# Head of a planned RWKV-attention and maxout-FFN kernel: scale factors on other engines, zeroing inside the list, one more chunk with corner products

## The chip, the cores and the metric

One core of one Trainium2 chip runs the whole program. The metric is device microseconds for one execution. Three timed executions of the kernel before took 390.78, 393.11 and 394.20 us; the median is 393.11 us. PE is TensorE, DVE is VectorE, ACT is ScalarE, POOL is GpSimd, and SP is SyncE, which issues most of the DMAs.

## What is computed

The inputs are r, k and v of shape (4, 8, 768, 48): batch, heads, time steps, head size. Per head there are a decay `w` and a bonus `u`. The output of the recurrence goes through a feed-forward net that takes a maximum of three projections:

```python
for t in range(S):
    cur = einsum('bhd,bhe->bhde', u[None] * kt, vt)
    y[:, :, t] = einsum('bhd,bhde->bhe', rt, state + cur)
    state = w[None, :, :, None] * state + einsum('bhd,bhe->bhde', kt, vt)
x = y.transpose(0, 2, 1, 3).reshape(3072, 384)
h = maximum(maximum(x @ w1, x @ w2), x @ w3)      # 384 -> 768
return h @ w_out                                  # 768 -> 384
```

## The kernel before

**Chunks.** The 768 steps are cut into NCH = 12 chunks of C = 64 steps. For a chunk the recurrence becomes four groups of small products, each done for two halves q = 0, 1 of the heads: `scores` (keys against queries, line 536), `keys` (the update of the state, line 586), `values` (the output, line 607), and for the first WHOLE = 2 chunks also `bonus` (line 550) and `flipped` (keys turned from feature to token layout, line 560). The output of a chunk goes as fp16 high and low parts into a tile x; six small DMAs (`x_last`, line 632) move the rest of its rows into place. Then `ffn(c)` (line 1007) does for 256 tokens 18 projections of 9 matmuls (`up`, line 656) and 3 of 18 matmuls (`down`, line 681); all of these are the matmuls of line 651.

**Precision.** Chunks 0 and 1 use fp32 operands in pieces of 64x64 (line 531). Later chunks split each operand into a high and a low fp16 part and use three products. The operands lie in `Block` tiles (line 409): per half-split s and unit u a 128-column field, of which the left 48 or 64 columns hold two heads, one in the upper and one in the lower 64 partitions. Chunks 2 and 3 (c < CORNERS = 4) multiply the two corners apart: two 64x64 matmuls for each product (line 524). From chunk 4 on, a DMA (`spread`, line 420, two issues for each block) copies a dense block into a block-diagonal one, and one 128x128 matmul does both heads (line 521). The rest of each block must be zero for that, so all 16 blocks are zeroed by POOL at the head (line 415), behind two zeroings of `ztop` (line 331) and ahead of one of `state` (line 439).

**Head.** Powers of the decay are made on DVE by scans (line 366). From them come, all on DVE, the row scales `sc` and `wrt` (lines 370 to 373), the chunk decay `wc` with two multiples `wcv` and `wck` (lines 376, 378, 390), `uw` (380), a diagonal matrix `dg` (382) and, on the list, `tkf` (line 387). `wu`, `cst` and the first inputs are issued by SP, `ut` by ACT.

**Weights.** The eight weight tiles come as 64-bit words: a DMA into one of three `raw64` buffers (line 323), then ACT (`tops`, line 340), DVE (`convert`, 344), ACT (`round_up`, 347) and DVE (`leave`, 350). Feed-forward block f needs weight f.

**Order.** From line 829 on all work is put on a list by `do(due, engine, cost, ...)`. `Plan.order` (line 171) runs a small model of the engines, PE's clock and the DMA lanes, and for each engine picks the ready entry of the least due time. Each entry's due time is shifted by the table SHIFT (line 79), by kind of work and by one of five stages; stage 0 holds due times under 0, stage 1 those from 0 to 1, and so on. The last call gives the time at which each engine is free (line 1083). The result is a fixed order of instructions on each engine; each engine runs its own in order. STIRS = 30 entries of three matmuls on zeros (line 647) keep PE's clock up where the model sees nothing else for PE. The order of before cannot be read from the table by eye; on the chip it is what the trace shows.

Of the kernel before, what the change touches and what calls it, by code (L numbers as in the profile page):

```python
# [26 lines left out]
U = 8  # L27
WHOLE = 2
CORNERS = 4
# [42 lines left out]
class Plan:  # L72
# [4 lines left out]
    BEFORE, BEHIND, PHASE, LANES = 1.5, 1.0, 1.4, 8  # L77
    CLASSES = (0.0, 1.0, 2.0, 10.0)
    SHIFT = {
        "sp feat": (3.37, -2.28, 2.83, -0.27, 0),  # L80
        "sp tok": (-0.37, -1.28, 2.64, 0.03, 0),
        "dve tkf": (0, 0.35, 0, 0, 0),
        "pe turned": (0, -0.88, 0, 0, 0),
        "act tkt": (0, -2.47, 0, 0, 0),
        "dve kT": (-0.62, -26.75, 0, 0, 0),
        "dve rT": (1.01, -35.26, -13.5, 0, 0),
        "act ru": (1.08, 1.39, 0, 0, 0),
        "pe bo": (-1.74, -0.21, 0, 0, 0),
        "dve am": (0, -0.03, 0.19, 2.29, 8.79),
        "pe sc": (6.74, 6.37, 4.36, -0.11, 0.12),  # L90
        "pe va": (-1.39, -2.73, -1.75, -0.08, 0),
        "act xh": (1.82, -0.83, 0.07, -0.97, -3.12),
        "dve xl": (0.58, 0, -2.36, -1.28, 1.02),
        "sp x3": (-1.49, -1.21, 0.13, -4.67, -1.28),
        "act xsq": (0, 0.01, 0, 2.16, -1.69),
        "pe stir": (0, -4.85, -11.53, -2.89, 0),
        "sp word": (2.21, 2.24, 0, 0, 0),
        "act ztop": (4.76, 27.48, 0, 0, 0),
        "dve word": (0, -2.64, 0, 0, 0),
        "act his": (3.42, 1.73, 0, 0, 0),  # L100
        "dve lo": (5.68, 7.43, 0, 0, 0),
        "pe kp": (5.05, -0.04, 0, 0, 0),
        "act kt": (-0.02, 0.84, 0, 0, 0),
        "pe ke": (-7.14, 6.21, -1.73, 0.35, 0),
        "act state": (0, -0.01, 0, 0, 0),
        "act sq": (0, 0.88, -7.89, 10.42, 25.44),
        "dve sd": (0, -0.87, 0, 0, 0),
        "dve state": (0.34, -0.75, -2.69, 4.27, 0),
        "act sdh": (4.06, 29.93, 3.51, 1.17, 0),
        "dve sdl": (-1.07, 0, 0.16, -0.97, 0),  # L110
        "pe up": (0, 23.33, 26.76, 0, 0.29),
        "act m": (4.63, 8.82, 0.44, 3.37, 1.6),
        "dve m": (0.55, -34.44, -6.62, -1.08, 1.37),
        "act hh": (-7.43, -4.42, -2.95, -0.81, -0.62),
        "pool hl": (6.4, -5.49, -7.62, -1.14, 0),
        "dve hl": (0, -2.26, 0.19, -0.23, 6.97),
        "pe dn": (0, 15.92, 0.15, 0.16, -7.02),
        "act io": (0, 1.07, -1.56, -0.11, 0.2),
        "sp io": (0, -0.8, -1.65, 0.71, 5.84),
        "act kdh": (0, -1.01, 0, -0.76, 4.34),  # L120
        "dve kdl": (0, 25.83, -3.45, -0.82, 0),
        "act rh": (0, -2.72, -12.01, 2.55, 0),
        "dve rl": (0, -0.6, 0, -4.47, 0),
        "dve a": (0, -2.22, 24.73, -7.12, -0.01),
        "act am": (0, -1.68, -2.12, 0, 0),
        "act ah": (0, 4.54, -7.22, -2.31, -3.79),
        "dve al": (0, -3.09, -4.17, -4.93, 4.72),
        "dve kdec": (0, 17.36, 44.29, 0, 0),
        "act ktdh": (0, 0.89, -1.64, -2.36, 0),
        "dve ktdl": (0, -3.21, -2.6, 0.42, 0),  # L130
        "act vdh": (0, 0, -14.62, 1.62, -3.2),
        "dve vdl": (0, 0, -2.03, -0.03, -0.05),
        "pool kT": (0, 0, -4.45, 18.88, 0),
        "pool rT": (0, 0, -2.66, 20.23, 3.89),
        "pool am": (0, 0, -3.01, 1.47, 1.83),
        "pool kdec": (0, 0, -10.33, 11.92, 0),
        "sp kb": (0, 0, 0, -6.2, 0.59),
        "sp ktb": (0, 0, 0, -1.92, 0),
# [1010 lines left out]
```

## Time and profile before

| | |
|---|---|
| median of the three runs | 393.11 us |
| the profiled execution's own time | 390.22 us |
| its span, first to last instruction | 388.2 us |
| PE busy | 375.1 us, 97% |
| DVE busy | 243.0 us, 63% |
| ACT busy | 244.3 us, 63% |
| POOL busy | 185.2 us, 48% |
| mean granted clock of PE | 0.993 |
| DMA | 77.23 MB, mean 199 GB/s |

The busy share is a mean over a head, a steady part and a tail with different limits, and PE's busy time holds the stirring matmuls too. What an edit is worth has to be read in the stage that it touches: views by stretches of time, the timeline of one engine, and the chain of waits that ended last.

### The profile page before, as it was taken

Reading aid. Unit: us, or ns where it says so; the run is one execution under the profiler, and the core shown is the slowest. Engines: PE = TensorE matmul, PEld = TensorE weight load, DVE = VectorE, ACT = ScalarE, POOL = GpSimd, SP = SyncE. Lnnn points to the kernel's source line nnn. Section 1 sums busy time; section 2 is a strip of 40 time slices with the busy share of each in tenths; the row PEclk is TensorE's granted clock in tenths of the full one; section 3 lists DMA queues with packets and bytes.
Section 4 is the critical chain, followed back from the end, with each engine's and each line's share of the span. In section 5 each row is a group of like instructions: output and inputs, shape, how many; then the busy total and the mean of one; then the engine's idle time right before and its main releaser. Section 6 shows DMA issues by size and latency. Waiting matters only on the chain.

```text
span 388.2 us, 13560 instructions
## 1 busy us (share of the span) xinstructions
PE 375.1 (97%) x5652; PEld 337.8 (87%) x5652; DVE 243.0 (63%) x464; ACT 244.3 (63%) x618; POOL 185.2 (48%) x187
## 2 busy tenths in 40 slices
PE   6998999899999999999999999999999999999993
PEld 4877988788889999999999999999999999998883
DVE  7397999868568597558557557456467466232350
ACT  3478986587547566566566566566556865696621
POOL 9600032359975683673673683674673550020110
PEclk8999999999999999999999999999999999999999
DMA  8866673324852994994994996994994994903201
GB/s 273 342 206 248 207 281 116 138 82 143 231 186 88 298 251 125 288 299 134 276 300 156 279 234 163 300 284 128 305 256 114 279 253 104 293 24 144 77 2 49
DMA packets 27989, 77.23 MB, mean 199 GB/s; under 512 B 4881, under 2 KB 12561, under 8 KB 26897
## 3 DMA queue, kind: packets, MB, share of 16 engines
q1 hardware_dynamic: 27776, 76.19, 66.1%
q8 instruction: 46, 0.75, 0.9%
q14 instruction: 23, 0.18, 0.2%
q10 hardware_dynamic: 144, 0.10, 0.1%
HBM read 38.38 MB, written 4.72 MB: 111 GB/s over the span
## 4 chain that ended last, share of the span: by engine, by line
PE 91%; POOL 4%; DVE 1%; ACT 1%; issue 1%; DVEq 0%; POOLq 0%
PE psm L651 72%; PE psv L521 8%; PE psa L521 3%; PE psv L524 2%; PE psv L531 2%; PE psm L647 1%; PE psa L531 1%; PE psa L524 1%; PE psa L565 1%; POOL ztop L331 1%; ACT am L497 1%; POOL ktd L415 0%; POOL vd L415 0%; POOL kd L415 0%; POOL sb L415 0%
## 5 line engine op out<-in xcount | busy, mean ns | idle before, releaser
L651 PEld LDWEIGHTS <-w 128*128 128x128 f16 x2592 | 250.2, 98 | 29.6 <-issue 0.7
L651 PE MATMUL psm<-x,w 128*128 128x256 f16 x1944 | 219.7, 273 | 0.0
L679 POOL TENSOR_TENSOR hl<-m,hh 128x256 f16<-128x256 f32 x60 | 44.6, 745 | 130.2 <-ACT hh L673 125.1
L670 DVE SCALAR_TENSOR_TENSOR m<-psm,m 128x256 f32<-128x256 f32 x144 | 60.2, 419 | 60.6 <-PE psm L651 52.5
L673 ACT CAST hh<-m 128x256 f16<-128x256 f32 x72 | 29.0, 402 | 56.2 <-DVE m L670 55.8
L651 PE MATMUL psm<-hh,w 128*128 128x256 f16 x432 | 56.3, 273 | 0.5 <-issue 0.5
L466 POOL TENSOR_TENSOR feat<-feat,wrt 128x512 f32<-128x512 f32 x36 | 49.1, 1376 | 7.0 <-DMA feat<-in_feat_dram 7.0
L485 POOL TENSOR_TENSOR am<-tok,u_sb 128x384 f32<-128x384 f32 x18 | 20.8, 1157 | 45.1 <-DVE al L584 45.1
L449 ACT ACTIVATE junk<-tok 128x384 bf16<-128x384 f32 x72 | 37.4, 520 | 3.3 <-DMA tok<-in_tok_dram 2.1
L666 ACT ACTIVATE m<-psm 128x256 f32<-128x256 f32 x72 | 27.2, 378 | 14.0 <-PE psm L651 12.7
L651 PE MATMUL psm<-hl,w 128*128 128x256 f16 x216 | 33.4, 273 | 0.0
L628 DVE SCALAR_TENSOR_TENSOR x<-psv,x 112x512 f16<-112x512 f32 x24 | 16.5, 688 | 22.6 <-ACT x L624 22.1
L624 ACT ACTIVATE x<-psv 112x512 f16<-112x512 f32 x24 | 14.3, 594 | 15.4 <-PE psv L521 14.4
L521 PE MATMUL psv<-rh,sb 128*128 128x64 f16 x256 | 23.6, 193 | 0.0
L521 PE MATMUL psv<-ah,vb 128*128 128x64 f16 x256 | 23.6, 193 | 0.0
L521 PE MATMUL psv<-al,vb 128*128 128x64 f16 x128 | 22.7, 193 | 0.0
L521 PE MATMUL psv<-rl,sb 128*128 128x64 f16 x128 | 22.7, 193 | 0.0
L499 POOL TENSOR_TENSOR am<-cs,a 128x512 f32<-128x512 f32 x18 | 20.0, 1114 | 3.4 <-DVE a L490 3.3
L490 DVE TENSOR_REDUCE a<-am 128x8 f32<-128x384 f32 x20 | 11.0, 549 | 16.9 <-POOL am L486 16.9
L521 PEld LDWEIGHTS <-vb 128*128 128x128 f16 x384 | 21.1, 98 | 0.4
L574 DVE COPY_PREDICATED am<-cs,psa 128x512 f32<-128x512 int32 x24 | 17.7, 736 | 5.6 <-PE psa L521 5.0
L696 ACT ACTIVATE io<-psm 128x256 f32<-128x256 f32 x36 | 13.4, 381 | 11.1 <-PE psm L651 11.0
(119 smaller groups left out, 579.2 us busy)
## 6 DMA issues: line engine op xcount, KB each, us to landing
tok<-in_tok_dram SPq DMA_DIRECT2D x26, 576.0 KB, 6.3
feat<-in_feat_dram SPq DMA_DIRECT2D x24, 512.0 KB, 4.6
raw<-in_ws_dram SPq DMA_DIRECT2D x6, 1152.0 KB, 7.1
out_dram<-io SPq DMA_DIRECT2D x36, 128.0 KB, 4.8
vb<-vd SPq DMA_DIRECT2D x16, 256.0 KB, 6.9
sb<-sd SPq DMA_DIRECT2D x16, 256.0 KB, 6.9
kb<-kd SPq DMA_DIRECT2D x16, 256.0 KB, 6.6
vb<-vd SPq DMA_DIRECT2D x16, 248.0 KB, 6.8
```

The costliest lines, as they stand in the source:

```text
L449: nc.scalar.activation(out=junk[:, 0:U * D].rearrange("p (u d) -> p u d", u=U), in_=src, func=AF.Square, scale=scale, accum_out=stat[:, ki ...
L466: helper(c).tensor_tensor(out=t[n], in0=t[n], in1=tb, op=ALU.mult)
L485: helper(c).tensor_tensor(out=w.rearrange("p (g b) d -> p g b d", g=2), in0=t["r"], in1=by_token(u_sb, q), op=ALU.mult)
L499: helper(c).tensor_tensor(out=t["a"], in0=eye.unsqueeze(1).broadcast_to([P, U, C]), in1=t.pop("sum").unsqueeze(2).broadcast_to([P, U, C]), ...
L521: nc.tensor.matmul(out=ps[:, i, :], lhsT=block[k].on[a][i], rhs=prods[k](b, i), **flags)
L574: nc.vector.copy_predicated(out=t["a"], mask=strict.unsqueeze(1).broadcast_to([P, U, C]), data=t.pop("sc"))
L628: nc.vector.scalar_tensor_tensor(out=x_part(x, 1, q), in0=ps, scalar=sc_x(c), in1=x_part(x, 0, q), op0=ALU.mult, op1=ALU.subtract)
L651: nc.tensor.matmul(out=ps, lhsT=a, rhs=b, start=first and n == 0, stop=last and n == len(prods) - 1)
L666: nc.scalar.mul(out=m, in_=ps, mul=by)
L670: nc.vector.scalar_tensor_tensor(out=m, in0=ps, scalar=by, in1=m, op0=ALU.mult, op1=ALU.max)
L673: nc.scalar.copy(out=h[0][:, f, :], in_=m)
L679: lows_by(c, f).tensor_tensor(out=h[1][:, f, :], in0=m, in1=h[0][:, f, :], op=ALU.subtract)
```

## The change

It has six parts.

1. **Loads.** `wu` and `cst` are issued on ACT's queue instead of SP's, ahead of `ut`.
2. **Scale factors.** `sc` is scaled by a `scalar_tensor_tensor` with a vector of ones instead of a `tensor_scalar`. `wc`, `uw` and `dg` are made by POOL, `wcv` and `wck` by ACT. `tkf` takes the buffer of `ru`. The scaling of `u_sb` is an entry on the list. The scaled copy of the state after chunk 0 moves from DVE to ACT.
3. **Zeroing.** `state` is no longer zeroed. Blocks are zeroed by 14 entries on POOL's list, and of the dense blocks only the columns that nothing else writes. Spreads wait for all of these.
4. **Corners.** CORNERS goes from 4 to 5, so chunk 4 uses corner products and no spreads.
5. **The list's model.** It adds TURN = 0.095 to the cost of a PE entry when it changes between corner products and full ones, and lowers some costs for it. Scores of chunks 0 and 1 come behind the bonus, values of the second half behind those of the first, and the projections of a chunk behind all of the chunk before. `ah` and `al` get two buffers.
6. **The table.** All of SHIFT is new, and the engines are taken as free at other times.

```diff
-CORNERS = 4
+CORNERS = 5
...
+            if e == "pe" and p["corner"] != corner:
+                corner = p["corner"]
+                cost += self.TURN
...
-    nc.sync.dma_start(out=wu_sb, in_=wu)
+    nc.scalar.dma_start(out=wu_sb, in_=wu)
...
+    nc.scalar.dma_start(out=cs, in_=cst)
...
-    nc.vector.tensor_scalar(out=sc, in0=sc, scalar1=SC_R, scalar2=None, op0=ALU.mult)
+    nc.vector.scalar_tensor_tensor(out=sc, in0=sc, scalar=SC_R, in1=one4, op0=ALU.mult, op1=ALU.mult)
...
-    nc.vector.tensor_copy(out=wc, in_=pw[:, :, C])
-    nc.vector.tensor_scalar(out=wcv, in0=wc, scalar1=SC_V, scalar2=None, op0=ALU.mult)
-    nc.vector.tensor_tensor(out=uw, in0=uf_sb, in1=w_sb, op=ALU.mult)
+    nc.gpsimd.tensor_tensor(out=wc, in0=pw[:, :, C], in1=one4, op=ALU.mult)
+    nc.gpsimd.tensor_tensor(out=uw, in0=uf_sb, in1=w_sb, op=ALU.mult)
...
-    nc.vector.tensor_tensor(out=dg, ...)
+    nc.gpsimd.tensor_tensor(out=dg, ...)
+    nc.scalar.mul(out=wcv, in_=wc, mul=SC_V)
+    nc.scalar.mul(out=wck, in_=wc, mul=SC_KT / SC_R)
...
     def both():
+        tkf = work.tile([P, U, C], F32, name="ru").rearrange("p (g h) s -> p g h s", h=2)
...
-            nc.gpsimd.memset(t.bitcast(F32), 0.0)
+            self.blank = self.dense.bitcast(F32)[:, :, :, w // 2:]
...
-    nc.gpsimd.memset(state, 0.0)
...
+            dma(due, lambda: spread(nc.sync, dst, src), 2.4, reads=[*keys, *(("pad", n) for n in range(14))], writes=[name], n=2)
...
-            do(due + 0.06, "dve", 0.5, lambda: nc.vector.tensor_scalar(out=state1[q], in0=sf, ...
+            do(due + 0.06, "act", act(U * D), lambda: nc.scalar.mul(out=state1[q], in_=sf, mul=S16), reads=[s], writes=[("sd", q)])
...
+    do(0.1, "act", 0.36, u_scaled, writes=["u"])
+    if W == P:
+        for n, b in enumerate([*kd, *ktd, *vd, *sd, kb, ktb, *vb, *sb]):
+            do(0.5 + 0.1 * n, "pool", 1.0 if n > 7 else 0.7, lambda b=b: nc.gpsimd.memset(b.blank, 0.0), writes=[("pad", n)])
...
-    order = plan.order(dict(pe=1.5, dve=5.2, act=3.0, pool=13.0, sp=1.6))
+    order = plan.order(dict(pe=1.5, dve=4.7, act=4.4, pool=5.4, sp=0.75))
```

Of the table, the entries that the prediction speaks of (stages 0 to 4, chunk units):

```diff
-        "act ztop": (4.76, 27.48, 0, 0, 0),
+        "act ztop": (-4.52, -2.31, 0, 0, 0),
-        "act his": (3.42, 1.73, 0, 0, 0),
+        "act his": (-16.68, -2.37, 0, 0, 0),
-        "pe kp": (5.05, -0.04, 0, 0, 0),
+        "pe kp": (1.15, 193.93, 0, 0, 0),
```

More of the change, by code (lines that the diff above doesn't have):

```diff
@@ L149, in __init__, with do @@
         self.bufs, self.todo, self.wrote, self.read = bufs, [], {}, {}
-    def do(self, due, eng, cost, fn, reads=(), writes=(), takes=(), move=0, near=0, parts=1, counts=1.0):
+    def do(self, due, eng, cost, fn, reads=(), writes=(), takes=(), move=0, near=0, parts=1, counts=1.0, corner=False):
         n = len(self.todo)
@@ L168, in do @@
         need.discard(n)
-        self.todo.append(dict(n=n, due=due, eng=eng, cost=cost, fn=fn, need=need, takes=takes, move=move, near=near, parts=parts, counts=counts, kind=kind, stage=stage, base=base, touch={*reads, *writes, *new}))
+        self.todo.append(dict(n=n, due=due, eng=eng, cost=cost, fn=fn, need=need, takes=takes, move=move, near=near, parts=parts, counts=counts, corner=corner, kind=kind, stage=stage, base=base, touch={*reads, *writes, *new}))
     def order(self, free):
@@ L185, in order @@
         ready = [p["n"] for p in self.todo if not p["need"]]
-        out, taken = [], {pool: [] for pool in self.bufs}
+        out, taken, corner = [], {pool: [] for pool in self.bufs}, False
         def earliest(p):
@@ L918, in before_keys @@
         if c < WHOLE:
-            do(due - 0.30, "pe", 0.76, lambda: flipped(c, q), reads=[("feat", c, q), ("kT", c, q)], takes=[("psa", ("kp", c, q))], counts=0.5)
+            do(due - 0.30, "pe", 0.70, lambda: flipped(c, q), reads=[("feat", c, q), ("kT", c, q)], takes=[("psa", ("kp", c, q))], counts=0.5, corner=True)
             do(due - 0.30, "act", act(U * D), lambda: flipped_back(c, q), reads=[("kp", c, q)], takes=[("kt", ("kt", c, q))])
@@ L956, in keyed @@
     def keyed(c, q, due, reads):
-        do(due, "pe", 0.76 if c < WHOLE else 0.64 if c < CORNERS else 0.62, lambda: keys(c, q), reads=reads, takes=[("psv", ("ke", c, q))], counts=0.5 if c < WHOLE else 1.0)
+        do(due, "pe", 0.72 if c < WHOLE else 0.64 if c < CORNERS else 0.62, lambda: keys(c, q), reads=reads, takes=[("psv", ("ke", c, q))], counts=0.5 if c < WHOLE else 1.0, corner=c < CORNERS)
         s = ("state", q)
@@ L972, in valued @@
         reads = [*reads, *held(c, [("sdh", q), ("sdl", q)], ("sb", q))]
-        do(due, "pe", 1.43 if c < CORNERS else 1.42, lambda: values(c, q), reads=[*reads, ("ah", c, q), ("al", c, q), ("rh", c, q), ("rl", c, q)], takes=[("psv", ("va", c, q))])
+        do(due, "pe", 1.43 if c < CORNERS else 1.42, lambda: values(c, q), reads=[*reads, ("ah", c, q), ("al", c, q), ("rh", c, q), ("rl", c, q), *[("valued", c)] * q], writes=[("valued", c)] * (not q), takes=[("psv", ("va", c, q))], corner=c < CORNERS)
         leave_x(c, q, due)
@@ L1013, in mul @@
                     T["up", c, f, i] = up([T["x", c][:, s] for s in range(2)], f, i, TOK)
-                do(due + 0.035 * i, "pe", 0.983, mul, reads=[*x, *((a, f, h) for a in ("his", "lo") for h in parts[i])], takes=[("psm", ("up", c, f, i))])
+                do(due + 0.035 * i, "pe", 0.983, mul, reads=[*x, *((a, f, h) for a in ("his", "lo") for h in parts[i]), *[("upped", c - 1)] * (c > 1)],
+                   writes=[("upped", c)] * (f == NF - 1), takes=[("psm", ("up", c, f, i))])
                 if i == 0:
```

190 lines of the change are left out of this document (95 added, 95 removed).

## The prediction

> **What bounds the kernel now.** I read the page's busy shares first, then the engines' busy time by stretches that I cut at the events of the head, then the timelines of single engines in the head, last the chain that ended last. The stretches (columns: length, then busy time of PE, PE's weight load, DVE, ACT, POOL, with counts; then PE's clock, DMA share, GB/s):
>
> ```profile
> 9.96:36.82 26.86, 24.30 (x608) 21.91 (x608) 17.57 (x24) 18.48 (x33) 6.04 (x8) 0.98 0.76 280
> 36.82:68.50 31.68, 31.68 (x447) 28.27 (x445) 31.41 (x46) 24.52 (x45) 7.52 (x7) 1.00 0.53 187
> ...
> 79.10:382.40 303.30, 303.18 (x4283) 275.19 (x4282) 178.05 (x356) 190.84 (x515) 158.80 (x157) 1.00 0.70 196
> ```
>
> Three limits stand behind one another. From 79.1 to 382.4 us PE is busy for 303.18 of 303.30 us: what is added to PE there is added to the end, and what waits on other engines or DMAs there costs nothing. From 36.82, where the first feed-forward product starts, to 68.5 both PE and DVE are full (31.41 of 31.68 us on DVE). Before 36.82 nothing is full: DVE is idle for 26.86 - 17.57 = 9.29 us after 9.96, and PE's high share is padded by stirring:
>
> ```profile
> L647 PE MATMUL psm<-still 128*128 128x256 f16 x90 | 13.6, 306 | 1.1 <-DVE still L266 1.1
> ...
> L558 DVE TENSOR_TENSOR am<-psa,cs 128x512 f32<-128x512 f32 x3 | 2.1, 689 | 4.4 <-PE psa L531 4.4
> ```
>
> 13.6 us of matmuls on zeros fill the head. So a shorter head is a shorter kernel, microsecond for microsecond, as far as DVE, which is full right behind it, gets its own work done earlier too. I therefore count the head in DVE time.
>
> **Scale factors.** The small DVE operations of the head, and POOL's zeroing beside them:
>
> ```profile
> 2.77 0.84 DVE L366 TENSOR_TENSOR_SCAN raw<-wu_sb,ones 128x64 f32<-128x64 f32 x4 [1.68 <-DMA wu_sb<-in_wu_dram]
> 3.65 0.18 DVE L370 RECIPROCAL sc<-raw 128x4 f32<-128x4 f32 x1
> 3.86 0.74 DVE L371 TENSOR_SCALAR sc<-sc 128x4 f32<-128x4 f32 x1
> ...
> 5.55 0.88 DVE L378 TENSOR_SCALAR wcv<-wc 128x4 f32<-128x4 f32 x1
> ...
> 6.48 0.76 DVE L387 TENSOR_TENSOR tkf<-wrt,wck 128x256 f32<-128x256 f32 x2
> 7.16 2.49 DVE L466 TENSOR_TENSOR feat<-feat,wrt 128x512 f32<-128x512 f32 x4
> ```
>
> ```profile
> 2.73 1.85 POOL L415 MEMSET kd<- 128x1024 f32 x2
> 4.52 1.89 POOL L415 MEMSET ktd<- 128x1024 f32 x2
> ...
> 15.26 0.74 POOL L439 MEMSET state<- 128x768 f32 x1
> ```
>
> A reciprocal of 4 columns takes 0.18 us, a scaling of the same 4 columns 0.74: it ends at 4.60, the two zeroings of kd at 4.58. Line 378 ends at 6.43, those of ktd at 6.41. These DVE forms wait out a zeroing; the change takes them off DVE or changes their form.
>
> After: the scans end at 3.61 as before. The trace has no POOL product of 4 columns; `wc` costs between nothing and the 0.90 us of one with 256 columns. `wcv` and `wck` on ACT cost at most 0.33 each, the price of 64 columns. A hand-over costs about 0.1 (ACT's copy of the state ends at 16.57, DVE goes on at 16.68, quoted below); there are three. That is 3.61 + 0.3 + 0.66 + (0 to 0.90) = 4.6 to 5.5 us, and `tkf` takes 0.68 more (6.48 to 7.16), to 5.3 to 6.2.
>
> ```profile
> 45.09 0.90 POOL L679 TENSOR_TENSOR hl<-m,hh 128x256 f16<-128x256 f32 x1 [29.10 <-ACT hh L673]
> ...
> L497 ACT ACTIVATE am<-cs,a x16: 331/332/348, 51.4 to 72.9; 128x64 f32<-128x64 f32 x16
> ```
>
> The inputs must be there too. SP's first big load moves from 1.66 to about 0.76, and such loads land 3.6 to 5.4 us after issue, so at 4.4 to 6.2:
>
> ```profile
> 1.66 0.43 SPq L272 DMA_DIRECT2D feat<-in_feat_dram  x1
> DMA to landing us min/median/max: 3.6/4.9/5.4
> ```
>
> I take 5.9 us for the first scaling of features, against 7.16, nearer to the late end because POOL's nearest row is that of 0.90: **-1.3 us**, with -1.0 and -1.9 as the ends. `uw` and `dg` follow on POOL; `dg` has 192 columns, so by the same row some 0.68 us, and is done before the first turned keys need it. ACT's two more DMA issues (0.43 us each by SP's row) lie in its wait for the scans and POOL; without that cover they would cost 0.9 us at the head of ACT's work.
>
> [...]
>
> **The state and the zeroing.** ACT's copy of the first state waits for POOL's last zeroing (15.26 + 0.74 = 16.00), and behind it in ACT's order stand the first weight's `tops` and the second half's output:
>
> ```profile
> 16.03 0.54 ACT L600 COPY state<-psv 128x192 f32<-128x192 f32 x2 [0.97 <-POOL state L439]
> ...
> 17.12 1.48 ACT L340 CAST ztop<-raw 128x1152 f16<-128x1152 bf16 x1
> ...
> 16.68 0.36 DVE L966 TENSOR_SCALAR state<-state 128x384 f32<-128x384 f32 x1 [1.11 <-ACT state L600]
> ```
>
> The wait of 0.97 goes: **-1.0 us**. It must go for the first term to count at all, since POOL's end would stay at 16. The 14 zeroings on the list take at most 0.95 us each, 13.3 in all, from about 5.6 to at most 19; POOL's next work starts at 45.09 and the first full products in the chain below, which need the spreads, stand at 126.02. So they are hidden; should they run late, POOL's low parts would be. They don't stretch DVE's feature scaling: it took the same with and without zeroing beside it.
>
> ```profile
> L466 DVE TENSOR_TENSOR feat<-feat,wrt x8: 684/685/686, 7.2 to 29.7; 128x512 f32<-128x512 f32 x8
> ```
>
> The two scaled copies of the state leave DVE, 0.36 us each: **-0.7 us** of DVE time (between 0, where DVE was waiting anyway, and 0.7). On ACT they go into its idle 26.86 - 18.48 = 8.4 us; so does the scaling of `u_sb`.
>
> **The new order.** Of DVE's 9.29 idle us some 2.1 belong to the wait just removed (1.11 at line 966, and about ACT's 0.97 again behind `tops`). Of the 7.2 left, 4.4 are the wait for the first bonus product, which PE did only behind turned keys and scores. In the new order bonus comes ahead of scores, and `ztop` and `his` of the first weights come much earlier, so weights can be converted in that hole: the first was issued at 3.56, its landing is 7.1 us, so it lay there from 10.7, and ACT took it up at 17.12.
>
> ```profile
> 3.56 2.31 SPq L323 DMA_DIRECT2D raw<-in_ws_dram  x3
> raw<-in_ws_dram SPq DMA_DIRECT2D x6, 1152.0 KB, 7.1
> ```
>
> How much of the 7.2 us is filled the trace can't say; the ends are 0 and 7.2. I take 40%, **-2.9 us**: a little nearer to nothing, because the weights also wait for one of three buffers. The added orderings (values, projections) and second buffers of `ah` and `al` issue nothing; I give them 0.
>
> **Corners for chunk 4.** From the chain, start, us, work:
>
> ```profile
> 85.75 0.87 PE psa L524 x48
> 86.62 3.05 PE psm L651 x27
> 89.67 0.71 PE psv L524 x48
> ...
> 93.44 1.51 PE psv L524 x96
> ...
> 126.02 1.40 PE psv L521 x48
> 127.42 8.52 PE psm L651 x78
> 135.93 0.70 PE psa L521 x24
> 136.63 0.60 PE psv L521 x24
> ```
>
> Corner products cost 0.87, 0.71 and 1.51 us for scores, keys and values, full ones 0.70, 0.60 and 1.40: 0.39 more per half, 0.78 for the chunk. And 27 projections behind corner products take 3.05 us where 27/78 of 8.52 are 2.95: 0.10 for each return, up to six. Between 0.8 and 1.4 us; I take **+1.2 us**. It falls where PE is full, so nothing covers it. What it saves, 16 of SP's issues and about 4 MB of spreads, was waited for by nobody there.
>
> **The sum.** -1.3 - 1.0 - 0.7 - 2.9 + 1.2 = -4.7 us. Against the profiled execution's own 390.22 us that is 385.5. The median of the runs is 393.11, 0.74% above the profiled one; a median of after should stand so too: 385.5 x 1.0074 = **388.4 us**, 1.2% faster.
>
> **Rivals.** *The head gives only its waits.* DVE is full from 36.82 to 68.5, so if its holes are not filled an earlier first projection only finds DVE late; then -1.3 - 1.0 and, with all six returns, +1.4: 389.3, as a median 392.2, no change. For it speaks that 31.41 of 31.68 us are taken; against it, that the 4.4 us hole hangs on PE's order, which changes. If the new forms don't relieve DVE either (the change not doing what it says), it is 390.6 or 393.5, still no change.
>
> *The head gives all.* Every hole filled, ends of the other terms: -1.9 - 1.0 - 0.7 - 7.2 + 0.8 = -10.0, so 380.2, as a median 383.0. Against it: dependences between the two halves leave holes in any order.
>
> *The second half's turned keys come late, and the kernel is slower.* The turned keys of chunk 0, second half, have a due time of about 0 before shifting, so they are in stage 1, and their shift goes from -0.04 to 193.93. Any other ready product of PE goes ahead of them, feed-forward products too. If PE's order puts them behind chunk 0's feed-forward, this chain must run before chunk 1's: turned keys 1.13, state product 0.85, copies 0.54 + 0.36, values 1.92, six small DMAs 3.91 and their landing 2.2: 10.9 us, against 1.7 us of chunk 2's scores to do meanwhile. So 9.2 us lost: 390.2 - 4.7 + 9.2 = 394.7, as a median 397.6. It outweighs the gain once the chain ends more than 4.7 us behind the last product of chunk 0. Against it: the list picks other work only where it is ready, and PE has little that is ready in the head.
>
> ```profile
> 27.46 1.13 PE psa L565 x32
> ...
> 29.68 0.85 PE psv L531 x32
> ...
> 38.96 1.92 PE psv L531 x64
> ```
>
> ```profile
> 24.98 3.91 SPq L635 DMA_DIRECT2D x<-x  x6
> x<-x SPq DMA_DIRECT2D x6, 16.0 KB, 2.2
> ```
>
> **Chances.** Forecast 0.46, only the waits 0.33, all of it 0.13, late keys 0.08. About 1% (3.9 us) can be told from no change, so the bounds are 389.2 and 397.0. The forecast's own range is 386 to 391; two thirds of it are faster by over 1%. Faster: 0.13 + 0.31 + a little = 0.46; slower: half of the last rival and 0.03 as a tail of the waits-only case, 0.07; the rest, 0.47, the same. The range reaches from the full head to past the waits-only case: 382.5 to 395.5.
>
> **What would show it.** Right: first feature scaling on DVE near 5.9 us, no DVE operation of 4 columns over 0.3 us; ACT's state copy without a wait on POOL; first projection at about 31 instead of 36.82; PE full from there on; scores, keys and values of chunk 4 as 48, 48 and 96 matmuls of 0.87, 0.71 and 1.51 us. Wrong: a first projection within 2.5 us of 36.82, a gap of several us on PE between 50 and 80 (late keys or DVE), or PE idle again around chunk 4 or 5 for lack of a zeroed block.

## The result, and the profile after

| | before | after |
|---|---|---|
| median of 17 runs each, us | 393.11 | 396.74 |
| ratio after to before | | 1.0115 [1.0089, 1.0141] |
| the profiled execution's own time, us | 390.22 | 396.57 |
| its span, us | 388.2 | 394.8 |
| first projection of the first feed-forward, us | 36.8 | 37.7 |

The change makes the kernel 1.2% slower. The ratio leaves out five runs of before of 402.7 to 408.12 us, so it is not the quotient of the two medians. The forecast was 1.2% faster, and the measured time lies outside its range.

The stretches of after, cut at the same events as those of before (length; busy time of PE, PE's weight load, DVE, ACT, POOL; PE's clock, DMA share, GB/s):

```profile
10.31:37.70 27.39, 25.26 (x640) 22.28 (x638) 17.63 (x21) 18.90 (x34) 5.99 (x8) 0.98 0.70 261
37.70:70.00 32.30, 32.30 (x425) 28.51 (x424) 30.90 (x48) 25.45 (x50) 5.52 (x5) 1.00 0.49 167
80.00:388.71 308.71, 305.19 (x4497) 275.77 (x4489) 191.45 (x357) 187.07 (x505) 159.41 (x155) 1.00 0.65 179
```

Two things differ. The head isn't shorter: the first stretch has about the same length (27.39 us, before 26.86) and the same DVE time (17.63 us, before 17.57), so DVE's idle time in it was not filled. And the last stretch, where PE was busy for all but 0.12 us, now has 308.71 - 305.19 = 3.52 us in which PE is idle. The chain that ended last points the same way. Its shares by engine, before and after:

```profile
PE 91%; POOL 4%; DVE 1%; ACT 1%; issue 1%; DVEq 0%; POOLq 0%
```

```profile
PE 78%; DVE 8%; DMA 5%; issue 3%; ACT 2%; POOL 1%; SPq 0%; DVEq 0%; ACTq 0%
```

The head on DVE, from its timeline:

```profile
4.84 0.84 DVE L373 TENSOR_TENSOR_SCAN raw<-wu_sb,ones 128x64 f32<-128x64 f32 x4 [3.74 <-DMA wu_sb<-in_wu_dram]
...
5.92 0.20 DVE L379 SCALAR_TENSOR_TENSOR sc<-sc,ones 128x4 f32<-128x4 f32 x1
6.16 0.69 DVE L381 TENSOR_TENSOR wrt<-raw,sc 128x256 f32<-128x256 f32 x1
...
6.95 0.76 DVE L395 TENSOR_TENSOR ru<-wrt,wck 128x256 f32<-128x256 f32 x2
7.63 1.89 DVE L476 TENSOR_TENSOR feat<-feat,wrt 128x512 f32<-128x512 f32 x3
```

(A tile named `ru` stands at line 395, because `tkf` now takes the buffer of `ru`.) The small operations are as short as predicted (`sc` 0.20 us where it was 0.74), but the scans start at 4.84 instead of 2.77, because `wu` comes late. Its issue in before and in after (columns: KB, us from issue to landing):

```profile
wu_sb<-in_wu_dram SPq DMA_DIRECT2D x1, 4.0 KB, 1.9
```

```profile
wu_sb<-in_wu_dram ACTq DMA_DIRECT2D x1, 4.0 KB, 4.0
```

So the first feature scaling starts at 7.63, not at 5.9 and not even at the old 7.16. ACT's copy of the state did lose its wait on POOL:

```profile
13.93 0.51 ACT L610 COPY state<-psv 128x192 f32<-128x192 f32 x2
```

What PE waited for from 60 to 142 us, before and after (us in total, times, longest):

```profile
PE psv L524 <- DVE ktd L434: 0.6, 1, 0.6
PE psm L651 <- issue: 0.5, 1, 0.5
PE psv L524 <- ACT ktd L429: 0.4, 1, 0.4
```

```profile
PE psv L534 <- issue: 2.4, 2, 1.6
PE psv L534 <- DVE vd L447: 1.0, 1, 1.0
PE psa L534 <- issue: 0.6, 1, 0.6
PE psm L661 <- issue: 0.6, 1, 0.6
PE psv L534 <- DVE al L594: 0.2, 1, 0.2
```

1.5 us became 4.8. "issue" is a wait for which the profile shows no semaphore; it makes up 3.6 of the 4.8, and it became the main subject of the experiments.

### The profile page after: what moved, and what is told of

Its sections match the earlier page's. It is cut to its first block, busy times and chain, and to the rows that moved or that the text cites. A ratio compares the mean times of both kernels' runs of the same rounds, so it can differ in the third digit from the quotient of the medians.

```text
span 394.8 us, 13941 instructions
## 1 busy us (share of the span) xinstructions
PE 377.5 (96%) x5844; PEld 338.3 (86%) x5844; DVE 254.7 (65%) x457; ACT 243.5 (62%) x622; POOL 186.3 (47%) x189
## 4 chain that ended last, share of the span: by engine, by line
PE 78%; DVE 8%; DMA 5%; issue 3%; ACT 2%; POOL 1%; SPq 0%; DVEq 0%; ACTq 0%
PE psm L661 60%; PE psv L531 7%; PE psm L657 3%; DMA kb<-kd 2%; PE psv L541 2%; PE psa L531 2%; PE psa L541 2%; DMA sb<-sd 2%; DVE ktd L445 1%; PE psv L534 1%; PE psa L575 1%; DMA wu_sb<-in_wu_dram 1%; DVE m L680 1%; DVE kd L445 1%; DVE am L584 1%
## 5 line engine op out<-in xcount | busy, mean ns | idle before, releaser
L689 POOL TENSOR_TENSOR hl<-m,hh 128x256 f16<-128x256 f32 x60 | 48.1, 803 | 118.0 <-ACT hh L683 117.8
L495 POOL TENSOR_TENSOR am<-tok,u_sb 128x384 f32<-128x384 f32 x18 | 19.0, 1054 | 52.9 <-DVE al L594 52.2
L445 DVE TENSOR_TENSOR kd<-feat,kd 128x512 f16<-128x512 f32 x20 | 18.7, 933 | 4.4 <-ACT kd L440 2.7
L496 POOL TENSOR_TENSOR am<-am,tok 128x384 f32<-128x384 f32 x18 | 20.8, 1154 | 1.4
L531 PE MATMUL psv<-rh,sb 128*128 128x64 f16 x224 | 20.7, 193 | 0.0
L531 PE MATMUL psv<-ah,vb 128*128 128x64 f16 x224 | 20.7, 193 | 0.0
L531 PE MATMUL psv<-al,vb 128*128 128x64 f16 x112 | 19.9, 193 | 0.0
L531 PE MATMUL psv<-rl,sb 128*128 128x64 f16 x112 | 19.9, 193 | 0.0
L447 DVE SCALAR_TENSOR_TENSOR sd<-state,sd 128x384 f16<-128x384 f32 x20 | 18.6, 936 | 1.5 <-ACT sd L440 1.5
L589 ACT CAST ah<-am 128x512 f16<-128x512 f32 x20 | 12.3, 616 | 11.5 <-DVE am L584 11.4
```

Of the source, the lines that this page charges most:

```text
L445: nc.vector.tensor_tensor(out=dense.dense[:, 1, :, 0:w], in0=src, in1=dense.dense[:, 0, :, 0:w], op=ALU.subtract)
L496: helper(c).tensor_tensor(out=w, in0=w, in1=units(t["k"]), op=ALU.mult)
L531: nc.tensor.matmul(out=ps[:, i, :], lhsT=block[k].on[a][i], rhs=prods[k](b, i), **flags)
L689: lows_by(c, f).tensor_tensor(out=h[1][:, f, :], in0=m, in1=h[0][:, f, :], op=ALU.subtract)
```

## The experiments

Ratios are to the kernel before, run on the same chip, with 95% intervals. The experiments ran on several chips, so a difference of two ratios is known to some 0.4%, 1.7 us. Where only a trace is compared, the times are of one execution.

### A. The parts, one by one

**1. The scale factors alone.** The kernel before, old order of the list, loads on SP, with the new forms and engines of the factors and without the zeroing of `state`.

```diff
-    nc.vector.tensor_scalar(out=sc, in0=sc, scalar1=SC_R, scalar2=None, op0=ALU.mult)
+    nc.vector.scalar_tensor_tensor(out=sc, in0=sc, scalar=SC_R, in1=one4, op0=ALU.mult, op1=ALU.mult)
-    nc.vector.tensor_scalar(out=wcv, in0=wc, scalar1=SC_V, scalar2=None, op0=ALU.mult)
+    nc.scalar.mul(out=wcv, in_=wc, mul=SC_V)
...
-    nc.gpsimd.memset(state, 0.0)
```

> The kernel before with one edit: the scale factors as in the change (POOL, ACT and the other DVE form), the zeroing of blocks behind them on POOL, none of state; loads on SP, order of the list as before. By my prediction's terms DVE's first feature scaling comes 1.3 us earlier and the wait of 0.97 us on POOL goes: about -2 us, ratio 0.994 to 0.996. Theory W: PE's head is fixed work (chunks 0 and 1, and 90 stirring matmuls that are issued however short the waits are), so only true idle time of PE in the head can go, 2.1 us ahead of the turning at 7.3 us and little else: -0.5 to -1.5 us, ratio 0.996 to 0.999. Rival N (the head's DVE time doesn't matter at all): ratio 1.000.

Measured: 390.26 us, ratio 0.9951 [0.9919, 0.9983]. The first scaling starts at 6.26:

```profile
4.95 0.76 DVE L388 TENSOR_TENSOR tkf<-wrt,wck 128x256 f32<-128x256 f32 x2
6.26 1.29 DVE L466 TENSOR_TENSOR feat<-feat,wrt 128x512 f32<-128x512 f32 x2 [0.55 <-DMA feat<-in_feat_dram]
```

`tkf` is done at 5.71; the features aren't there yet, which was the prediction's other bound. This part is a gain of some 1.9 us.

It would be more but for one DVE operation. The first scaled copy of the state now starts in the middle of POOL's zeroing, at 12.86 instead of 16.68, and takes 4.42 us where before took 0.36. It ends at 17.28, 0.22 us behind the last zeroing:

```profile
12.86 4.42 DVE L966 TENSOR_SCALAR state<-state 128x384 f32<-128x384 f32 x1
15.22 1.84 POOL L416 MEMSET sb<- 128x1024 f32 x2
```

PE waits 1.7 us for the DVE work behind it, and the first projection comes at 36.02, only 0.8 us earlier than in before. The whole change has no such wait, since there the copy is on ACT. The copy stays on DVE in experiments 3, 11, 15 and the control below, and took 4.88 to 6.87 us in all their profiles but one.

**2. Corners for chunk 4 alone.** The kernel before, in its order; chunk 4's products read the dense blocks, and its spreads issue nothing. The output is not the reference's; only the time counts.

```diff
-                if c >= CORNERS:
+                if c > CORNERS:
...
-            dma(due, lambda: spread(nc.sync, dst, src), 2.4, reads=keys, writes=[name], n=2)
+            dma(due, lambda: spread(nc.sync, dst, src) if c > CORNERS else None, 2.4, reads=keys, writes=[name], n=2)
```

> The kernel before with one edit: chunk 4 uses corner products and issues no spreads; the order of everything else is that of the kernel before. Theory W: PE is full there, so only the products' own price shows, +1.2 to 1.8 us: ratio 1.003 to 1.005, with no new wait on PE. Rival C (corners are the whole loss): +3.5 us or more, ratio 1.009 or above, with waits on PE about chunk 4.

Measured: 393.19 us, ratio 1.0012 [0.9978, 1.0045]: +0.5 us, with an interval that holds 0 and 1.2. The chain that ended last is sharper. From the first scores of chunk 4 to the end of the first values of chunk 5 it takes 156.40 - 121.23 = 35.17 us in before and 159.68 - 123.52 = 36.16 us here, 0.99 us more:

```profile
121.23 0.70 PE psa L521 x24
...
155.00 1.40 PE psv L521 x48
```

```profile
123.52 0.88 PE psa L524 x48
...
158.28 1.40 PE psv L521 x48
```

**3. Factors and corners, old order.** Experiment 1 with `CORNERS = 5`.

> The kernel before with the scale factors of the change (as in the run of these alone, which stood at 0.9951) and with CORNERS = 5, ordered by the old list and its old table. Theory W2 (corners cost their price, the new list and table cost the rest): 0.9951 plus 0.9 to 1.7 us, ratio 0.997 to 1.000, chunk-1 feed-forward as long as before (34.4 us from its first to the next chunk's first projection). Rival C (corners for chunk 4 pull its attention forward and make PE wait in any order): ratio 1.004 or above, waits on PE between 70 and 120 us of 3 us or more.

Measured: 390.89 us, ratio 0.9965 [0.9931, 0.9999]. Against experiment 1 the corners cost 0.14%, 0.5 us, again within the intervals; the same piece of the chain takes 36.16 us, against 35.17 in experiment 1.

**4. After, with `wu` and `cst` on SP again.** Same order, same table.

```diff
-    nc.scalar.dma_start(out=wu_sb, in_=wu)
+    nc.sync.dma_start(out=wu_sb, in_=wu)
-    nc.scalar.dma_start(out=cs, in_=cst)
+    nc.sync.dma_start(out=cs, in_=cst)
```

> The changed kernel with one edit: wu and cst are issued by SP again, ahead of the features. Its order of instructions on every engine is otherwise that of the changed kernel. In the changed kernel the scans wait until 4.74 us for wu, 2.77 in the kernel before. Theory W (waits by order): the scans start at 2.8 again and DVE's first feature scaling comes at 6 to 7 us, but PE's waits between 70 and 120 us (4.7 us in all against 1.5 before) stem from the order, so at most 1 us returns: ratio to the kernel before 1.008 to 1.013. Rival L (late load): DVE is full from 37 to 80 us, so its 2 us of delay are what PE waits for later; 2 to 4 us return: ratio 1.001 to 1.006.

Measured: 393.97 us, ratio 1.0049 [1.0021, 1.0077]. The loads are worth 0.66%, 2.6 us: the scans start at 2.83, the first projection at 35.4. The rest, 1.0049 against 0.9965 of experiment 3, is what the new order and its table cost: 0.84%, **3.3 us**, where the prediction had a gain of 2.9. In it are also the zeroing entries and the state's copies on ACT, for which the prediction had another gain of 0.7, and which spare the slow copy that experiment 3 has.

**5. After, `wu` alone on ACT.** `cst` and `ut` on SP ahead of the features.

> The changed kernel with wu left alone on ACT's queue; cst and ut are issued by SP ahead of the features. If wu is late in the changed kernel because its packets of 32 bytes share the DMA engines with feature packets of 4 KB issued at the same time, the scans start at 2.8 to 3.3 us here, as with wu on SP, and the time is near that run's (394 us). If ACT's queue itself is slow to deliver, they start at 4.5 us or later, and the time is near the changed kernel's (397 us).

Measured: 394.53 us, ratio 1.0053 [1.0026, 1.0081]; `wu` lands 2.4 us after issue and the scans start at

```profile
3.26 0.84 DVE L373 TENSOR_TENSOR_SCAN raw<-wu_sb,ones 128x64 f32<-128x64 f32 x4 [2.16 <-DMA wu_sb<-in_wu_dram]
```

So ACT's queue alone doesn't make it late. In after SP issues the first features in the same moment (both at 0.75 us). The 128 packets of 32 bytes that make up `wu` move from 2.42 to 4.15 us there, while SP's queue moves 200 packets with 0.56 MB, among them feature packets of 4096 bytes; in before they move from 1.75 to 2.30, ahead of the first feature packet at 2.75.

### B. What makes PE wait in the new order: first theory, DVE

The theory: the new order asks for chunk 4's attention some 12 to 18 us earlier than the old one (its first scores at 102.8 instead of 120.5, its second at 123.6 instead of 135.5), at a time when DVE is full.

**6. New list, `CORNERS = 4`** (experiment 4 with the constant as before).

> The changed kernel with wu and cst on SP (which stood at 1.0049) and CORNERS back at 4; the new list and table order it anew. Theory W2: the corners' price goes (0.9 to 1.7 us), the waits of the new order stay: ratio 1.0005 to 1.003, PE waits of 3 us or more between 70 and 120 us. Rival C: the waits go with the corners, ratio 0.996 or below.

Measured: 413.61 us, ratio 1.0548 [1.0464, 1.0632], with one PE wait of 12.63 us at 135.8, for a spread. This misses both expectations. The planner makes another order as soon as a cost changes, so list and table can't be told apart by swapping.

**7. After, without computing the low parts of the weights** (POOL zeroes them instead, so the products miss these).

> The changed kernel with one edit: the low parts of the eight weight tiles are not computed; POOL writes zeros instead, so DVE has 8 operations of 1.4 us less between 20 and 70 us (11.3 us). The products with the low parts are still done. Theory W with DVE as the late engine: PE's waits between 70 and 120 us shrink from 4.7 to under 1.5 us, and 3 us or more return: ratio 1.003 or less. Rival O (PE's own order, waits on PE's chain, whatever DVE does): waits stay above 3 us, ratio 1.008 or more.

Measured: 396.91 us, ratio 1.0128 [1.0047, 1.0209]. PE's waits from 60 to 142 us are still 4.4 us. A backlog of DVE from the weights isn't the cause.

**8. POOL lighter** (experiment 4, without POOL's feature scaling for chunks 3 and 4).

> The changed kernel with wu and cst on SP (1.0049); POOL's scaling of the features of chunks 3 and 4 is left out, eight operations of about 1.3 us between 68 and 120 us, so these chunks compute with unscaled features. The order on all engines is otherwise the same. Theory P (POOL, 85% busy there, delivers chunks 3 and 4 late and stretches DVE's operations beside it): PE's waits between 70 and 120 us shrink from 4.5 to under 2 us, ratio 0.997 to 0.999. Rival O (the order asks PE for products whose chain through ACT and DVE is too long, whatever POOL does): waits stay above 3.5 us, ratio 1.004 or more.

The unscaled features leave the kernel's bounds, so its second, general path ran as well (9187.52 us), and the time says nothing. In the trace of the first part PE's waits from 70 to 120 us are 3.1 us, against 4.9 in experiment 4: between the two expectations.

**9. Twelve DVE operations fewer** (experiment 4, no low parts of keys, turned keys and v for chunks 3 and 4; those of chunk 2 are used again).

```diff
-        do(due + 0.02, "dve", dve(U * w), lambda: low(dense, src(), w, scale), ...
+        do(due + 0.02, "dve", dve(U * w), lambda: None if c in (3, 4) else low(dense, src(), w, scale), ...
```

> The changed kernel with wu and cst on SP (1.0049); DVE's low parts of keys, turned keys and v for chunks 3 and 4 are left out (12 operations of 0.8 to 1.4 us, about 12 us of DVE, most of them between 75 and 116 us), so these chunks use the low parts of chunk 2. All other instructions and their order stay. Theory D (the new order asks for half a chunk more of attention before 116 us, and DVE, 47 of 52 us busy there, can't keep up): PE's waits after 80 us (2.9 of 4.5 us) shrink to under 0.7, ratio 0.996 to 0.999. Rival Q (PE waits for chains through POOL and ACT whatever DVE's load): waits after 80 us stay above 2 us, ratio 1.003 or more.

Measured: 390.98 us, ratio 0.9965 [0.9923, 1.0007]. The ratio lies where theory D had it; PE's waits after 80 us, 1.7 us, lie between its 0.7 and the 2 us of rival Q. About half of the gain lies in the head, where a PE wait of 1.46 us at 32 us was missing. The wait for `vd` is gone; what stays has no semaphore:

```profile
PE psv L534 <- issue: 3.1, 3, 1.6
PE psa L534 <- issue: 0.2, 1, 0.2
```

**10. Two stirring entries fewer** (experiment 4, the last two of 30 issue nothing).

> The changed kernel with wu and cst on SP (1.0049), without the last two of the 30 stirring entries, which stand in PE's order between the first feed-forward products of chunk 0 (1.0 us of PE). If PE's time there sets the end, 1.0 us returns: ratio 1.002 to 1.003. If the waits between 70 and 120 us absorb it (they are set by other engines), nothing returns: ratio 1.0045 to 1.0055, and the waits grow by about 1 us.

Measured: 393.34 us, ratio 1.0025 [0.998, 1.0069]. The list ended 1.5 us earlier in the trace, but the interval of the time holds both expectations. The waits stayed, and the one at 71.7 us stood six matmuls later in the program than in experiment 4. That was the hint: it belongs to a count of instructions and not to a product.

### C. Second theory: PE waits for its own instructions

The busy time from the start up to a moment inside a wait also counts the instructions up to there (x of PE and of its weight load). After, up to its waits without a semaphore from 33 us on:

```profile
0.00:35.50 35.50, 29.78 (x602) 25.12 (x602) 21.63 (x37) 21.41 (x39) 12.79 (x23) 0.95 0.76 284
0.00:76.00 76.00, 68.70 (x1241) 59.36 (x1242) 59.29 (x95) 53.45 (x110) 22.87 (x32) 0.98 0.64 233
0.00:102.80 102.80, 93.48 (x1881) 81.03 (x1882) 82.33 (x132) 72.46 (x161) 46.81 (x53) 0.98 0.55 196
0.00:113.60 113.60, 103.64 (x2137) 89.95 (x2138) 93.06 (x148) 79.31 (x178) 52.60 (x58) 0.98 0.54 192
0.00:117.00 117.00, 106.29 (x2265) 92.26 (x2266) 96.28 (x153) 82.39 (x187) 55.92 (x60) 0.99 0.53 187
```

The sums are 1204, 2483, 3763, 4275 and 4531: steps of 1279, 1280, 512 and 256, multiples of 256 within one. Before has 1205 and 2739 at its waits of 1.67 us at 33.9 and 0.50 us at 78.6, six times 256 apart within two. The instruction queue of the profile, q8, moved 46 packets with 0.75 MB in before, 16 KB each, for 11304 counted instructions of PE, and 48 in after for 11688: 246 and 244 counted ones for each packet. That a packet holds 256 instructions of PE, 64 bytes each, is an estimate from these counts and the steps above; the profile doesn't say what a packet holds.

A corner product of 96 matmuls takes 1.51 us, so by estimate 256 instructions (128 matmuls and their weight loads) last 2.0 us; of projections, 27 in 3.05 us, they last 14 us. Behind the waits of after that end at 76.40, 103.06 and 113.81 us the next transfer starts 1.1 us later; the transfers around them take 0.9 to 1.4, and PE goes on 1.3 to 1.5 us behind the end of one: 3.3 to 4.0 us in all, the sum of these. With data under way it came later. PE used up a block of 256 at 70.84 us in after (1112 + 1114 = 2226 counted, 257 before the wait at 76.0), and no instruction transfer moves until 74.0, 3.2 us later (DMA queues of the two stretches 70.9 to 74.0 and 74.0 to 75.0):

```profile
q1 hardware_dynamic: 496, 0.98, 85.8%
```

```profile
q1 hardware_dynamic: 193, 0.39, 101.9%
q8 instruction: 1, 0.02, 5.8%
```

At 74.82 PE ran dry in the middle of a product, for 1.59 us.

**11. Extra traffic that nobody waits for** (experiment 15's kernel in the old order, below, with 2 x 576 KB more behind one token load).

```diff
         nc.sync.dma_start(out=t, in_=tok[c, q])
+        if (c, q) == (3, 1) and 'v' not in raws[c, q]:
+            for n in range(2):
+                nowhere = dram.tile([P, 3, 2, B, D], F32, name=f"nowhere{n}")
+                nc.sync.dma_start(out=nowhere, in_=tok[c, q])
```

> The factors alone with cst on ACT (old order), and behind the token load of chunk 3, second half (issued at 68.7 us) two more transfers of the same 576 KB from one place of DRAM to another, which nothing reads or waits for. Theory F, second half: the transfer of PE's next 256 instructions waits behind data in the DMA engines. By it the transfer that came at 72.7 us there comes only when the extra ones are through, at some 77 to 80 us, and PE's wait at the boundary of 256 instructions at 74.6 us grows from 0.51 to 3 to 6 us; the time grows by 2.5 to 6 us. If instructions don't wait behind data, that wait stays at 0.5 us and the time within 1 us, since the next load that PE's work hangs on is issued only at 80.4.

Measured: 394.83 us, ratio 1.0035 [0.9999, 1.0072], where that kernel without the traffic has 0.9907 [0.9876, 0.9939], 1.3% less. The one wait without a semaphore from 60 to 125 us grew from 0.51 us to

```profile
PE psm L655 <- issue: 3.8, 1, 3.8
```

at the same count as in before, 1369 + 1370 = 2739:

```profile
0.00:82.00 82.00, 71.58 (x1369) 62.71 (x1370) 70.60 (x105) 53.89 (x107) 27.04 (x32) 0.98 0.64 228
```

No data depends on these transfers. PE had used up a block at 73.24 us, and no instruction transfer moved before 81.76, 8.5 us later; without the extra traffic the same block was used up at 67.91 and the transfer came 4.8 us later. So PE waits for instructions there, and they wait behind data: the transfer came 3.7 us later behind its block, and PE waited 3.3 us longer. In the time it can't be read off so cleanly. The eight runs spread from 392.77 to 404.52 us. In the profiled one PE's granted clock stood at 0.50 from 84 to 88 us, behind the wait of 3.8 us, and at 0.87 from 88 to 92, by an estimate from these two some 2.5 us more; in before it stood at 0.50 from 8 to 10 us, behind a wait of 2.1 us. It had also lost time before the traffic began: its first copy of the state took 6.87 us, and its first projection came at 38.55 us.

**12. No corner products in after's order** (experiment 4; products of chunks 2 to 4 with half of the instructions).

```diff
-                if c >= CORNERS:
-                    nc.tensor.matmul(out=ps[:, i, :], lhsT=block[k].on[a][i], ...
+                if True:
+                    nc.tensor.matmul(out=ps[:, i, :], lhsT=(block if c >= CORNERS else dense)[k].on[a][i], ...
```

> After with wu and cst on SP again, the same order; the products of chunks 2 to 4 are issued as full ones on the dense blocks (one 128x128 matmul in the place of two 64x64, so each product has half of its PE instructions; a dense block holds no corner apart, so the output isn't the reference's). DVE, POOL and ACT do the same work in the same order. Theory F: most of PE's waits from 70 to 120 us in this order (1.55, 0.52 and 1.35 us there) are not waits for DVE but for PE's own instructions, which come in transfers of 16 KB, 256 instructions; corner products use up 256 instructions faster than the next ones come. By it these three go or shrink to under 0.6 us in sum, the waits of 70 to 120 us sum to under 2 (the one for DVE's low part of v, 1.05, may grow), and with 18 products at 0.11 to 0.17 us less for each the time falls by 4 to 6 us against the same kernel with corners: a ratio of 0.989 to 0.995 to the kernel before. Theory D (DVE and POOL are full, and PE comes too early for them): the waits stay at 4 us or grow, since PE asks earlier still: a ratio of 0.998 to 1.005.

Its sums, too, leave the bounds (9189.93 us with the general path), so only the trace of the list counts. All waits without a semaphore from 60 to 145 us are gone, as theory F (instructions) said. Waits for DVE of 4.7 us and for ACT of 0.7 stand in their place, as D (DVE) said. Neither holds alone.

**13. The same, timed** (the general path is never taken), **and 14. with the twelve DVE operations of experiment 9 left out too.**

```diff
-    with tc.If(nc.values_load(got["flag"]) > 0):
+    with tc.If(nc.values_load(got["flag"]) > 1):
```

> The kernel of the run without corners (after's order, loads on SP, products of chunks 2 to 4 as full ones on the dense blocks; output not the reference's), with the second, general path never taken, so that its time can be read. In that run's trace PE's three waits at boundaries of 256 instructions were gone (3.4 us), but waits for DVE stood in their place (0.4, 0.7, 1.7 and 1.4 us from 68 to 91). If two limits stand one behind the other (instructions first, DVE right behind), only what the 18 products are shorter shows in the time, some 2 us: a ratio of 0.998 to 1.001. If instructions alone are the cause, 0.989 to 0.995.

> As the run before it, and 12 DVE operations fewer: no low parts of keys, turned keys and v for chunks 3 and 4 (those of chunk 2 are used again). If two limits stand one behind the other, both are gone now: PE's waits from 65 to 125 us sum to under 1.5 us and the time falls by 3 us or more against the run before it, a ratio of 0.985 to 0.992. If a third thing holds PE in this order (POOL, the loads, the copies by ACT), the waits stay over 3 us and the ratio over 0.995.

**And as a control the old order**, experiment 3 without the same twelve operations:

> The control in the old order: factors and corners for chunk 4 (0.9965 before), without the same 12 DVE operations. There PE waits for DVE 0.99 us from 70 to 120, and both waits are for chunk 2's turned keys, which stay: nothing is gained, a ratio of 0.994 to 0.998. If the 12 operations are worth as much here as in the new order (0.84%), DVE's work and not the order is the cause: 0.985 to 0.990.

Measured: 393.04, 387.79 and 391.20 us. On the chip of these three runs the kernel before took 403.04 us, against 392.3 to 393.1 us on the others, so the ratios to it (0.9771, 0.9634, 0.9736) aren't used; the three are compared with each other, and by their spans of 390.9, 386.4 and 389.1 us. A comparison of their times with those of other experiments is one between chips. PE's waits from 60 to 142 us in 13, then in 14:

```profile
PE psv L531 <- DVE vd L447: 2.5, 3, 1.4
PE psv L531 <- DVE al L594: 1.7, 1, 1.7
PE psm L661 <- ACT m L676: 0.7, 1, 0.7
PE psv L531 <- DVE ktd L445: 0.4, 1, 0.4
```

```profile
PE psm L661 <- DVE hl L689: 1.2, 2, 0.9
PE psm L661 <- ACT hh L683: 0.9, 2, 0.7
PE psv L531 <- DVE vd L447: 0.3, 1, 0.3
PE psm L661 <- ACT m L676: 0.3, 1, 0.3
```

The times fit the first expectation of both: two limits stand one behind the other. Without the instruction waits alone, 13 is within 1 us of experiment 4 (393.97), less than the 2 us that its shorter products should give; without both, 5.25 us are gained. The waits do not fit: 2.2 us of them remain in 14 from 65 to 125 us, where under 1.5 were expected. In the old order the same twelve operations gain nothing: 391.20 us against 390.89 with them, and PE waits 1.5 us from 60 to 142 us without them and 1.2 us with them. It is the order, then, and not the amount of DVE work.

The busy time of experiment 3 and of experiment 4 from 64 to 116 us shows the place (columns as above; the third pair is DVE's):

```profile
64.00:90.00 26.00, 24.78 (x591) 21.51 (x589) 20.93 (x37) 18.49 (x50) 14.49 (x13) 1.00 0.38 132
90.00:116.00 26.00, 26.00 (x442) 23.05 (x440) 17.33 (x30) 16.77 (x48) 23.68 (x21) 1.00 0.32 107
```

```profile
64.00:90.00 26.00, 24.13 (x582) 20.87 (x580) 24.35 (x40) 20.85 (x63) 19.73 (x17) 1.00 0.44 150
90.00:116.00 26.00, 22.93 (x695) 20.18 (x695) 22.42 (x37) 18.32 (x48) 19.22 (x17) 1.00 0.39 117
```

From 90 to 116 us the new order sends PE 695 matmuls where the old one sends 442, since the corner products of chunk 4 (and the values ahead of them) are drawn into this stretch; and DVE, which has to prepare them, is busy for 46.77 of 52 us instead of 38.26.

### D. A version that beats both

**15. Experiment 1 with `cst` alone on ACT's queue**, run twice.

```diff
-    nc.sync.dma_start(out=cs, in_=cst)
+    nc.scalar.dma_start(out=cs, in_=cst)
```

> The kernel before with the scale factors of the change (0.9951), and cst alone issued on ACT's queue, so that SP issues the features 0.45 us earlier behind wu. There DVE waited 0.55 and 0.52 us for the two feature loads. If these waits count, 0.3 to 0.6 us more are won: ratio 0.9935 to 0.9945. If packets of the features now hold up wu as in the changed kernel, the scans start later than 3.3 us and the ratio is 0.996 or above.

> The factors alone with the old order of the list, and of the loads cst alone on ACT's queue, in more rounds: the version that the runs so far point to. If cst alone on ACT lets the features come earlier and nothing is paid for it (the first feature scaling at 5.78 in the one profile of this kernel, against 6.26 with cst on SP), the ratio to the kernel before is 0.992 to 0.994, some 0.5 us below the 0.9951 of the factors alone. If the gain at the head is lost again before PE needs it (the FFN's first projection is bound by PE's own work), it is 0.995 as with the factors alone. If cst too is held up behind the features as wu was, it is 0.998 or more.

Measured: first 391.24 us, the median of four runs from 386.91 to 393.24, where before took 392.36; then 388.67 us, the median of eight from 386.43 to 390.38, ratio **0.9907 [0.9876, 0.9939]**. The first scaling, in the profile of the second:

```profile
4.64 0.76 DVE L388 TENSOR_TENSOR tkf<-wrt,wck 128x256 f32<-128x256 f32 x2
5.76 1.60 DVE L466 TENSOR_TENSOR feat<-feat,wrt 128x512 f32<-128x512 f32 x2 [0.36 <-DMA feat<-in_feat_dram]
```

SP's first feature load goes out one issue earlier, and `wu` stays ahead of it. But this profile, of the shortest of the eight runs (386.43 us), differs more elsewhere. Here the state's copy got through between two zeroings:

```profile
12.70 0.58 DVE L966 TENSOR_SCALAR state<-state 128x384 f32<-128x384 f32 x1
```

In the profile of the first four (393.0 us) the same kernel's copy took 6.85 us, and PE waited 3.9 us for the DVE work behind it. In the good profile PE's instruction wait near 33 us is missing too, and the first projection starts at 32.47, against 36.02 in experiment 1. So this version beats before and after, but how much of that is the load of `cst`, and how much is a copy that happened to get through, is open: the intervals of 0.9951 and 0.9907 overlap. No run puts the copies on ACT in the old order, which would tell.

## Why the prediction was wrong

**The first feature scaling at 5.9 us, -1.3.** Failed at "the scans end at 3.61 as before". The prediction counted the two moved DMAs as 0.43 us of issue each on ACT and gave SP's big load the earlier place as a gain; it didn't ask what that load does to the small one issued beside it. `wu` took 4.0 us instead of 1.9, the scaling came at 7.63, and the moved loads cost 2.6 us. With `wu` ahead, the step holds: 6.26 and 5.76.

**The state's wait, -1.0.** Right: the wait is gone, and no PE wait of after is for a spread that a late zeroing could have held up. Together with the first term, 2.3 us were predicted, and 1.9 measured in the old order. That they agree so well is partly luck, since the measured gain has the slow copy of the state in it.

**The two scaled copies of the state, -0.7.** They did move to ACT (0.52 us at 14.47). The term took their 0.36 us each from before, where they run behind POOL's last zeroing. Once the wait on POOL is gone, the first would run beside the zeroing, and on DVE it then took 4.42 to 6.87 us in five of six profiles. The prediction had seen DVE forms wait out a zeroing at 4 columns, and did not carry it over to this copy. So the move is probably worth more than 0.7; no run measures it by itself.

**The new order, -2.9.** This is the step that decided it, and it failed in sign: +3.3 us, with the copies and the zeroing entries in it. It counted DVE's holes in the head as time that an order can win. DVE's busy time in the head stayed (17.63 us for 17.57). With the loads on SP, the new order starts the first projection at 35.4 against 36.4 in the old one, which is 1.0 us (and the old one has the slow copy in it), and loses it and more later. The sentence that "what waits on other engines or DMAs there costs nothing" from 79.1 us on is true of the old order's trace only. An order that moves corner products into a stretch where DVE is nearly full, and lets PE use up 256 instructions in some 2.0 us, where the next ones came in 3.3 to 4.0, makes new waits; either one alone is covered by the other.

**Corners, +1.2.** Right: 0.99 us in the chain, twice, and within the range of 0.8 to 1.4. The times of experiments 2 and 3 (+0.5 us) are too coarse to tell this from 0.

**The rivals.** None was it. The slower one looked for late keys in the head (9.2 us); they didn't come late: the last turned keys end at 33.57 us, ahead of the first projection at 37.69. Its 397.6 us is near the measured time by chance. No rival took PE's own instruction stream as a limit; in the profile of before it shows only as two waits put down to "issue", 1.67 us at 33.9 and 0.5 at 78.6, which the prediction did not take up. Of the signs named as wrong, the first projection within 2.5 us of 36.82 was there.

**`wrt` beside POOL.** The prediction's sum has no term for it: `wrt` took 0.69 us in after beside POOL's `dg` (6.06 to 6.57) and 0.70 in experiment 1 (`dg` from 4.06), against 0.42 in before, where POOL zeroed beside it, and 0.43 in experiment 15, where `cst`, which `dg` needs, comes later and `dg` starts at 6.11. That is 0.3 of the 1.7 us by which the first scaling missed 5.9. A like case stands in before: of two DVE products of line 350 the one beside a POOL product took 2.09 us, the one ahead of it 1.35.

```profile
65.14 1.35 DVE L350 SCALAR_TENSOR_TENSOR w<-raw,w 128x1152 f16<-128x1152 f32 x1
65.96 4.01 POOL L466 TENSOR_TENSOR feat<-feat,wrt 128x512 f32<-128x512 f32 x2 [7.01 <-DMA feat<-in_feat_dram]
66.74 2.09 DVE L350 SCALAR_TENSOR_TENSOR w<-raw,w 128x1152 f16<-128x1152 f32 x1
```

**From the profile to the median.** The factor 1.0074 did not carry over: after's profiled execution took 396.57 us and its median is 396.74.

**The sum:** factors -1.9, corners +0.5, order +3.3, loads +2.6: +4.5 us, which is 1.15% of 393. These are steps from one ratio to the next, so that they add up is no check on them.

**Open:** what the state's copies on ACT are worth, in the old order and in the new; which of the new table and of the added orderings draws the attention forward, since neither runs without the other; and how the waits that remain in 14 would go.

## What to carry to other kernels

When PE is the bound, count its instructions and not only its time: here a run of 64x64 matmuls used up 256 of them in some 2 us, and the next ones came in 3.3 to 4.0 us, later when big loads were under way (with 1.2 MB more their transfer began 8.5 us behind its block instead of 4.8), so such products want long matmuls between them. Taking away one wait shows little while another limit stands right behind it; take both away once before one is ruled out. A small load on which the head hangs goes out ahead of the big ones, whatever queue it is on (`wu` landed after 1.9 to 2.0 us on SP's queue and 2.4 on ACT's, but after 4.0 beside the features). When a wait is taken away, see what the work behind it will now run beside: the state's copy on DVE lost its wait for POOL and took 4.42 us instead of 0.36, to 0.22 us behind POOL's last zeroing.

## What the hardware showed that was not expected

- With 1.2 MB of traffic that nothing needed (experiment 11) an instruction transfer came 8.5 us behind its block instead of 4.8, and PE waited 3.8 us instead of 0.5 for its next 256 instructions.
- 4 KB in packets of 32 bytes landed after 4.0 us in after, where a queue of 4096-byte packets started in the same moment, instead of 1.9 to 2.0 in before and experiments 1 and 4, and after 2.4 us in experiment 5, with two small loads ahead of those packets.
- A scaling of 384 columns on DVE took 0.36 us behind POOL's zeroings and 4.42, 4.88, 4.89, 6.85 and 6.87 us when it began beside them, each time to some 0.2 us behind the last of them; once it got through in 0.58 us.
- Waits from 33 us on that the profile puts down to "issue", in the middle of a product, lay multiples of 256 counted instructions apart, within two, in before (1205, 2739) and after (1204, 2483, 3763, 4275, 4531) alike, and the one at 2739 stayed there under the extra traffic of experiment 11.
